# Attention with its gradient: the key-side gradient Z of two key groups in the halves of one bank, four units of a block turned on TensorE, ScalarE's order written out, new lists

## The chip, the cores and the metric

The kernel runs on one core of one Trainium2 chip. The metric is the device time of one execution in microseconds (us); three runs of the kernel before gave 2305.57, 2306.34 and 2306.37. Engines are called PE (TensorE; PEld is its weight load), ACT (ScalarE), DVE (VectorE), POOL (GpSimd) and SP (SyncE, which here mostly issues transfers).

## The reference

A block of a transformer, forward and backward, in bfloat16: sequence 2048, width 512, 32 heads of 16. The part that the change touches is attention.

```python
q, k, v = qkv[0], qkv[1], qkv[2]
scores = jnp.einsum("bhqd,bhkd->bhqk", q, k) * (Dh ** -0.5)
p = _softmax(scores, axis=-1)
o = jnp.einsum("bhqk,bhkd->bhqd", p, v)
...
_out, _vjp = jax.vjp(_f, A_x, A_wqkv, A_wo, B_w1, B_b1, B_w2, B_b2)
_grads = _vjp(grad_out)
```

Around it stand a layer norm, a gated MLP and the gradients of all weights; the kernel computes those ahead of attention and behind it.

## The kernel before

**The three parts.** A first part (up to about 157 us, and then mixed into the first block of attention) prepares operands. Attention runs to about 1949 us. A last part computes the weight gradients.

**Attention's loop.** Heads are taken in 16 pairs, and the 2048 queries in 4 groups of 512: 64 blocks. A block walks over the keys in 16 *steps* of 128 keys (`g` counts steps over all blocks, `kb = g % 16`), and both heads of the pair (`hj`) are done side by side. In one step, with the names of the lists:

- `s`: PE computes the scores, keys on partitions, two matmuls of 32 contraction rows each, in a buffer of two PSUM banks (L1058). `S`: ACT takes the exponential, which gives `et` (L1086).
- `d0`, `d1`: PE computes the output gradient times V for the first and the second head (L1080), each into a bank of its own. `m0`, `m1`: DVE multiplies each by `et`, which gives the halves of `gts` (L1097).
- `a1`, `a2`: PE accumulates in X (one bank, 128 partitions) what the queries need: from `et` with Lc and NAT (L1117, L1120; four matmuls of 32 columns each, in the four column quarters of the array), and from `gts` (L1130; two, in the upper two quarters).
- Every two steps SP issues a transfer that transposes `gts` into `gk` (L1106).

When a block's steps are done, DVE copies X to `xs`, PE transposes it (`XT`, L1142), DVE copies it out (`xt`), and `sm` (`emit_finish`) computes with small operations on DVE (rL, dl, ndr: L1163, L1166, L1168) and Pool (L1158 to L1179) the matrices W1 and W2 and the rows of the output and of dQ.

Then follows the key side, Z, for that block, while the next block's steps run. It needs the exponentials with queries on partitions, in 16 *units* (a group of 512 keys, `kc`, times a group of 128 queries, `qb`). There are two ways to get them. In 13 of the 16, PE computes the scores again, the other way round (`t`, L1070), and ACT takes the exponential (`T`, L1091). In the other three (`turned=(0, 1, 2)`: the unit `qb == 3` of the key groups 0, 1 and 2) PE transposes parts of four `et` (`E`, L1042: 8 transposes of 128x128) and DVE copies them out (`eE`, L1047), so ACT has nothing to do. `ze` and `zg` then multiply with W1 and W2 and add up in Z (L1190, L1198): two matmuls each, of 128 rows and 32 columns, in column quarters 0 and 1. Z has 64 partitions and one bank and holds 512 keys; after its four `qb`, DVE adds it to `acc` (L1213, L1215) or, in the last query group, writes the sum to `ob` (L1217), which SP stores (L1219).

**What sets the order.** PE, ACT and DVE each run a list. `PE_ORDER` and `DVE_ORDER` are written out by hand for one block; an item such as `d1:5` is the operation and its step relative to the block, and `unrolled` repeats the list with the step moved on by 16. For `t`, `T`, `ze`, `zg` and `acc` the number counts units, and units 16 to 31 belong to the block of steps 0 to 15. ACT's list is made by a loop: S, then T, of each number. The first block has its own lists (`first_block`), with the rest of the first part between its items. Each engine runs its list strictly in order, and waits for what the next item needs.

**Where items meet.** `s` and `t` share two buffers of two banks (pool `ps_st`), so the n-th of them on PE waits for ACT to finish the one two earlier. `d0` and `d1` have one buffer each, so each waits for the product of the step before. XT, E and Z all use the one bank of the tag `z` (pool `ps_z`): each *tenant* must be copied out by DVE before PE writes the next. `et` has 8 buffers, `gts` 4 (two steps each), `gk` 6 (four steps each).

Of the kernel before, what the change touches and what calls it, by code (L numbers as in the profile page):

```python
# [944 lines left out]
a2:-1 zg:-7 d1:1 t:1 ze:-6 s:2 d0:1 zg:-6 ze:-5 zg:-5 t:2 d1:2 a1:0 s:3 d0:2 XT:-1 d1:3 s:4 a1:1 a1:2 t:4 d0:3 a2:0 ze:-4  # L945
a2:1 zg:-4 a2:2 ze:-3 s:5 d1:4 zg:-3 ze:-2 t:5 d0:4 zg:-2 ze:-1 zg:-1 s:6 d1:5 a1:3 a1:4 d0:5 t:6 E:3 s:7 a1:5 d0:6 s:8
d1:6 ze:0 a2:3 zg:0 ze:1 a2:4 t:8 d1:7 zg:1 s:9 d0:7 d1:8 ze:2 a2:5 d0:8 t:9 zg:2 s:10 d1:9 ze:3 a1:6 zg:3 t:10 d0:9 a1:7
a1:8 s:11 d1:10 E:7 s:12 d0:10 a1:9 d1:11 t:12 a1:10 a2:6 ze:4 a2:7 s:13 d0:11 zg:4 d1:12 a2:8 ze:5 d0:12 t:13 zg:5 a2:9
ze:6 a2:10 d1:13 s:14 d0:13 zg:6 a1:11 d1:14 t:14 a2:11 ze:7 zg:7 s:15 d0:14 a1:12 a2:12 d1:15 t:15 E:11 s:16 d0:15 a1:13
d1:16 t:16 a1:14 a2:13 ze:8 a2:14 zg:8 s:17 d0:16 a1:15 ze:9  # L950
"""
DVE_ORDER = """
m0:-5 m1:-4 m0:-4 m1:-3 m0:-3 m1:-2 acc:-9 m0:-2 m1:-1 eE:-5 m0:-1 m1:0 m0:0 xs:-1 m1:1 m0:1 acc:-5 m1:2 m0:2 xt:-1 m1:3
m0:3 sm:-1 m1:4 m0:4 acc:-1 m1:5 m0:5 eE:3 m1:6 m0:6 m1:7 m0:7 m1:8 m0:8 m1:9 acc:3 m0:9 m1:10 eE:7 m0:10 m1:11
# [14 lines left out]
def attention_core(ctx, tc, opnds, ps_z, tail, NAT_s, NATQ_s, Oall, dQall, dKVT_out, ident_f32, ident_bf, npairs=16, nqc=4, turned=(0, 1, 2)):  # L969
# [4 lines left out]
    nc = tc.nc  # L974
# [4 lines left out]
    etp = ctx.enter_context(tc.tile_pool(name="etp", reuse_waits="tile", bufs=8))  # L979
    gtp = ctx.enter_context(tc.tile_pool(name="gtp", reuse_waits="tile", bufs=4))  # L980
    gbp = ctx.enter_context(tc.tile_pool(name="gbp", reuse_waits="tile", bufs=6))
    ep = ctx.enter_context(tc.tile_pool(name="ep", reuse_waits="tile", bufs=8))
    eep = ctx.enter_context(tc.tile_pool(name="eep", reuse_waits="tile", bufs=4))
# [38 lines left out]
    st_s = {}; st_d = {}; st_t = {}; st_et = {}; st_e = {}; st_gts = {}  # L1022
# [6 lines left out]

    def b_unit(g):  # L1030
        j = g // 16 - 1
        return (j, (g % 16) // 4, g % 4) if 0 <= j < NB else None

    def is_turned(kc, qb):
        return kc in turned and qb == 3

    def emit_E(g):

        ET = ps_z.tile([128, 2, 512], bf16, name="ET", tag="z")
        for hj in range(2):  # L1040
            for m in range(4):
                nc.tensor.transpose(ET[:, hj, m * 128:(m + 1) * 128], st_et[g - 3 + m][:, hj, 384:512], ident_bf[:])  # L1042
        cur["ET"] = ET

# [28 lines left out]
    def emit_d(g, hj):  # L1073
        j, kb = divmod(g, 16)
        p, qc = blocks[j]
        op = cur_op[p]
        d = ps_d.tile([128, 512], f32, name=f"d{hj}", tag=f"d{hj}")
        st_d[g, hj] = d
        r = slice(64 + 32 * hj, 96 + 32 * hj)
        nc.tensor.matmul(d[:], lhsT=op["KVT"][r, kb * 128:(kb + 1) * 128], rhs=op["QDT"][r, qc * 512:(qc + 1) * 512],  # L1080
                         start=True, stop=True, tile_position=(64 + 32 * hj, 0))
# [11 lines left out]
    def emit_mult(g, hj):  # L1093
        if g // 2 not in st_gts:
            st_gts[g // 2] = gtp.tile([128, 2, 2, 512], bf16, name="gts")
        gts = st_gts[g // 2]
        nc.vector.tensor_tensor(out=gts[:, g % 2, hj], in0=st_d.pop((g, hj))[:], in1=st_et[g][:, hj], op=ALU.mult)  # L1097
# [52 lines left out]
    def emit_finish(j):  # L1150
# [12 lines left out]
        nc.vector.reciprocal(out=rL[:], in_=XTv[:, :, 2:4, 17:18])  # L1163
        nc.gpsimd.tensor_tensor(out=W1[:, :, :, 0:16], in0=ndo, in1=rL[:].to_broadcast([128, 4, 2, 16]), op=ALU.mult)  # L1164
        dl = finp.tile([128, 4, 2, 1], f32, name="dl")
        nc.vector.tensor_tensor(out=dl[:], in0=XTv[:, :, 2:4, 0:1], in1=rL[:], op=ALU.mult)  # L1166
        ndr = finp.tile([128, 4, 2, 1], f32, name="ndr")
        nc.vector.scalar_tensor_tensor(out=ndr[:], in0=dl[:], scalar=-1.0, in1=rL[:], op0=ALU.mult, op1=ALU.mult)  # L1168
# [5 lines left out]
        nc.gpsimd.tensor_tensor(out=t1[:], in0=XTv[:, :, 0:2, 0:16], in1=dl[:].to_broadcast([128, 4, 2, 16]), op=ALU.mult)  # L1174
        nc.gpsimd.tensor_tensor(out=t1[:], in0=XTv[:, :, 2:4, 1:17], in1=t1[:], op=ALU.subtract)
# [6 lines left out]

    def emit_ze(g):
        j, kc, qb = b_unit(g)
        if qb == 0:
            cur["Z"] = ps_z.tile([64, 512], f32, name="Z", tag="z")
        Z = cur["Z"]
        e = st_e.pop(g)
        for hj in range(2):
            nc.tensor.matmul(Z[32 * hj:32 * hj + 32, :], lhsT=blk[j]["W1"][:, qb, hj, :], rhs=e[:, hj, :],  # L1190
                             start=(qb == 0), stop=False, tile_position=(0, 32 * hj))

    def emit_zg(g):
        j, kc, qb = b_unit(g)
        gk = blk[j]["Gk"][kc]
        for hj in range(2):
            grhs = gk[:].rearrange("q a (r h b) k -> q a r h b k", r=2, h=2)[:, :, :, hj, qb, :]
            nc.tensor.matmul(cur["Z"][32 * hj:32 * hj + 32, :], lhsT=blk[j]["W2"][:, qb, hj, :], rhs=grhs,  # L1198
                             start=False, stop=(qb == 3), tile_position=(0, 32 * hj))

    def emit_acc(g):
        j, kc, qb = b_unit(g)
        p, qc = blocks[j]
        Z = cur.pop("Z")
        if kc == 0:
            if qc == 0:
                cur["acc"] = accp.tile([64, S], f32, name="acc")
            if qc == nqc - 1:
                cur["ob"] = outp.tile([64, S], bf16, name="ob")
        ks = slice(kc * 512, (kc + 1) * 512)  # L1210
        acc = cur["acc"]
        if qc == 0:
            nc.vector.tensor_copy(out=acc[:, ks], in_=Z[:])  # L1213
        elif qc < nqc - 1:
            nc.vector.tensor_tensor(out=acc[:, ks], in0=Z[:], in1=acc[:, ks], op=ALU.add)  # L1215
        else:
            nc.vector.tensor_tensor(out=cur["ob"][:, ks], in0=Z[:], in1=acc[:, ks], op=ALU.add)  # L1217
            if kc == 3:
                nc.sync.dma_start(out=dKVT_out[p * 64:(p + 1) * 64, :], in_=cur["ob"][:])  # L1219
        if kc == 3:  # L1220
            blk[j].pop("Gk")
# [3 lines left out]
    def turned_step(g):  # L1225
        return g % 16 % 4 == 3 and g % 16 // 4 in turned

    def unrolled(order):
        items = [x.split(":") for x in order.split()]
        items = [(k, int(r)) for k, r in items]  # L1230
        late = ("t", "T", "ze", "zg", "acc")
        return [(k, 16 * b + r) for b in range(-2, NB + 3) for k, r in items
                if (16 if k in late else 0) <= 16 * b + r < (NSTEP + 16 if k in late else NSTEP)]

    def first_block():

# [36 lines left out]
    def needs(k, g):  # L1273
        if k == "V":
            return [("eE", g - 1)] if ("E", g - 1) in issued else []
# [14 lines left out]
        if k in ("E", "XT"):  # L1290
            return [("S", g) if k == "E" else ("xs", g)] + ([before[k, g]] if (k, g) in before else [])
# [4 lines left out]
        if k in ("m0", "m1"):  # L1296
            return [("S", g), ("d" + k[1], g)]
        return {"acc": [("zg", g)], "xs": [("a1", g), ("a2", g)], "xt": [("XT", g)], "sm": [("xt", g)],
                "eE": [("E", g)], "zg": [("ze", g)]}[k]

    def emit_left(g, place):
        for f, a in left[g][place]:
# [148 lines left out]
```

## Time and profile before

| | us |
|---|---|
| median of three runs | 2306.34 |
| the profiled execution | 2310.21 |
| its span, first to last instruction | 2308.3 |
| first `s` to first XT | 157.3 to 214.3 |
| first XT to last XT (64 of them) | 214.3 to 1932.3 |
| last store of `ob` issued | 1949.1 |
| mean of one `d`, product, S, T, E transpose | 0.384, 0.684, 1.043, 1.042, 0.221 |

A group of instructions in the profile has a line, an engine, an operation, the tiles out and in, their shapes, how often it occurred, the engine's busy time in it, the mean of one, and the idle time ahead of it with what ended it. Means are of single instructions; since an engine starts the next one before the last is finished, the pace at which they follow one another is shorter, and is read from the timeline (start, duration, engine, line, operation, tiles). In the table by stages, "PEclk" is the clock that TensorE was granted, as a share of its full clock, and "DMA share" the mean busy share of the transfer engines, counted by packets, so that it can exceed 1.

### The profile page before, as it was taken

The page shows a single profiled execution, that of the slowest core. Times are in us where ns is not written, and L with a number is a line of the kernel's source. Part 1 is how long each engine was busy: PE and PEld are TensorE (multiplying, and loading weights), DVE is VectorE, ACT ScalarE, POOL GpSimd, SP SyncE. Part 2 cuts the span into 40 slices and gives each one's busy share as a digit, 9 for nine tenths or more (in the row PEclk, how much of TensorE's full clock was granted, in tenths as well). Part 3 has the DMA queues.
Part 4 walks back from the last instruction along what each step waited for, and adds up shares of the span by engine and source line. Part 5 has one row for each costly group of instructions (what it writes and reads, how often), then busy time and mean ns, then how long its engine had stood idle before and what let it go on. Part 6 is the DMA issues. An engine that isn't in the chain of part 4 may idle for free.

```text
span 2308.3 us, 50925 instructions
## 1 busy us (share of the span) xinstructions
PE 2227.2 (96%) x20089; PEld 797.6 (35%) x20135; DVE 2040.3 (88%) x3612; ACT 2030.4 (88%) x2322; POOL 345.4 (15%) x808
## 2 busy tenths in 40 slices
PE   7988999999999999999999999999999998799999
PEld 3432333333333333333333333333333333344544
DVE  7767999999999999999999999999999996788355
ACT  7667999999999999999999999999999997586243
POOL 4321111111111111111111111111111112310000
PEclk9999999999999999999999999999999999899999
DMA  9888899999999999999999999999999897987872
GB/s 293 273 271 177 157 181 164 185 163 183 162 180 166 179 165 179 167 177 173 171 177 167 175 168 181 164 185 162 179 166 179 157 159 183 259 184 153 129 202 71
DMA packets 1311407, 413.46 MB, mean 179 GB/s; under 512 B 1272416, under 2 KB 1286368, under 8 KB 1310528
## 3 DMA queue, kind: packets, MB, share of 16 engines
q1 hardware_dynamic: 1302880, 391.99, 90.7%
q0 software_dynamic: 4368, 12.98, 1.7%
q10 hardware_dynamic: 3920, 5.24, 0.7%
q8 instruction: 157, 2.57, 0.5%
q14 instruction: 82, 0.67, 0.1%
HBM read 44.42 MB, written 49.03 MB: 40 GB/s over the span
## 4 chain that ended last, share of the span: by engine, by line
PE 81%; DVE 11%; ACT 3%; DMA 3%; issue 2%; SPq 0%; POOL 0%; DVEq 0%; ACTq 0%; POOLq 0%
PE d L1080 12%; PE X L1117 11%; PE s L1058 11%; PE Z L1198 9%; PE X L1130 7%; DVE gts L1097 5%; PE Z L1190 5%; PE ET L1042 5%; PE t L1070 4%; PE ps_dw L783 2%; PE ps_dy L866 2%; PE XT L1142 2%; PE X L1120 1%; PE ps_dhg L799 1%; PE ps_dwkv L899 1%
## 5 line engine op out<-in xcount | busy, mean ns | idle before, releaser
L1097 DVE TENSOR_TENSOR gts<-d,et 128x512 bf16<-128x512 f32 x2048 | 1321.8, 684 | 73.1 <-issue 22.0
L1086 ACT ACTIVATE et<-s 128x1024 bf16<-128x1024 f32 x1024 | 1042.9, 1043 | 7.6 <-PE d L1080 7.1
L1091 ACT ACTIVATE e<-t 128x1024 bf16<-128x1024 f32 x832 | 866.1, 1042 | 24.9 <-PE t L1070 6.0
L1080 PE MATMUL d<-QDT,KVT 32*128 32x512 bf16 x2048 | 757.2, 384 | 20.2 <-DVE gts L1097 15.7
L1058 PE MATMUL s<-QDT,KVT 32*128 32x512 bf16 x2048 | 398.2, 385 | 2.5 <-ACT et L1086 2.0
L1198 PE MATMUL Z<-gk,W 128*32 128x512 bf16 x2048 | 397.5, 385 | 0.0
L1117 PE MATMUL X<-et,Lc 128*32 128x512 bf16 x2048 | 370.0, 389 | 0.0
L1120 PE MATMUL X<-et,NAT 128*32 128x512 bf16 x2048 | 369.0, 388 | 0.0
L1130 PE MATMUL X<-gts,NAT 128*17 128x512 bf16 x2048 | 330.7, 381 | 0.0
L1190 PE MATMUL Z<-e,W 128*32 128x512 bf16 x1664 | 321.8, 383 | 3.9 <-DVE ob L1217 1.2
L1070 PE MATMUL t<-KVT,QDT 32*128 32x512 bf16 x1664 | 323.6, 383 | 1.0 <-ACT e L1091 1.0
L1080 PEld LDWEIGHTS <-KVT 32*128 32x128 bf16 x2048 | 172.9, 90 | 232.3 <-issue 231.9
L1164 POOL TENSOR_TENSOR W<-NATQd,rL 128x128 bf16<-128x128 bf16 x64 | 25.8, 403 | 1122.7 <-DVE rL L1163 1122.7
L1058 PEld LDWEIGHTS <-KVT 32*128 32x128 bf16 x2048 | 105.9, 91 | 250.8 <-issue 231.2
L1198 PEld LDWEIGHTS <-W 128*32 128x32 bf16 x2048 | 100.4, 95 | 173.3 <-issue 143.0
L1190 PEld LDWEIGHTS <-W 128*32 128x32 bf16 x2048 | 105.3, 94 | 107.9 <-issue 97.3
L1070 PEld LDWEIGHTS <-QDT 32*128 32x128 bf16 x1664 | 92.2, 91 | 145.7 <-issue 141.1
L1117 PEld LDWEIGHTS <-Lc 128*32 128x32 bf16 x2048 | 83.5, 93 | 162.7 <-issue 162.6
L1047 DVE COPY eE<-ET 128x1024 bf16<-128x1024 bf16 x192 | 130.2, 678 | 4.5 <-PE ET L1042 4.4
L1042 PE MATMUL ET<-ident_bf,et 128*128 128x128 bf16 x1536 | 119.4, 221 | 2.1 <-DVE e L291 2.1
L1042 PEld LDWEIGHTS <-et 128*128 128x128 bf16 x1536 | 86.8, 98 | 45.7 <-issue 45.7
L1130 PEld LDWEIGHTS <-NAT 128*17 128x17 bf16 x2048 | 79.6, 89 | 59.7 <-issue 43.3
(213 smaller groups left out, 2354.2 us busy)
## 6 DMA issues: line engine op xcount, KB each, us to landing
gk<-gts SPq DMA_TRANSPOSE x512, 4.6
H1T_s<-h1p SPq DMA_DIRECT2D x28, 256.0 KB, 4.7
h<-H1T_s SPq DMA_DIRECT2D x28, 256.0 KB, 3.6
HGT_s<-hgT SPq DMA_DIRECT2D x21, 256.0 KB, 4.3
NAT_s<-NS SPq DMA_DIRECT2D x4, 1056.0 KB, 5.3
dKVT_s<-ob SPq DMA_DIRECT2D x16, 256.0 KB, 3.5
gb<-GB_s SPq DMA_DIRECT2D x8, 512.0 KB, 5.2
Rkv<-dKVT_s SPq DMA_DIRECT2D x2, 2048.0 KB, 10.2
```

The source lines that it names most:

```text
L1042: nc.tensor.transpose(ET[:, hj, m * 128:(m + 1) * 128], st_et[g - 3 + m][:, hj, 384:512], ident_bf[:])
L1058: nc.tensor.matmul(s[:, hj, :], lhsT=op["KVT"][r, kb * 128:(kb + 1) * 128], rhs=op["QDT"][r, qc * 512:(qc + 1) * 512], start=True, stop=Tr ...
L1070: nc.tensor.matmul(t[:, hj, :], lhsT=op["QDT"][r, q0:q0 + 128], rhs=op["KVT"][r, kc * 512:(kc + 1) * 512], start=True, stop=True, tile_pos ...
L1080: nc.tensor.matmul(d[:], lhsT=op["KVT"][r, kb * 128:(kb + 1) * 128], rhs=op["QDT"][r, qc * 512:(qc + 1) * 512], start=True, stop=True, til ...
L1086: nc.scalar.activation(out=et[:], in_=st_s.pop(g)[:], func=ACT.Exp)
L1091: nc.scalar.activation(out=e[:], in_=st_t.pop(g)[:], func=ACT.Exp)
L1097: nc.vector.tensor_tensor(out=gts[:, g % 2, hj], in0=st_d.pop((g, hj))[:], in1=st_et[g][:, hj], op=ALU.mult)
L1117: nc.tensor.matmul(X[64 + 32 * hj:96 + 32 * hj, :], lhsT=Lc[:, :], rhs=et[:, hj, :], start=(kb == 0), stop=False, skip_group_check=True, t ...
L1120: nc.tensor.matmul(X[32 * hj:32 * hj + 32, :], lhsT=NATt[:, kb, hj, 1:33], rhs=et[:, hj, :], start=(kb == 0), stop=(kb == 15), tile_positi ...
L1130: nc.tensor.matmul(X[64 + 32 * hj:64 + 32 * hj + 17, :], lhsT=NATt[:, kb, hj, 0:17], rhs=gts[:, kb % 2, hj, :], start=False, stop=(kb == 1 ...
L1190: nc.tensor.matmul(Z[32 * hj:32 * hj + 32, :], lhsT=blk[j]["W1"][:, qb, hj, :], rhs=e[:, hj, :], start=(qb == 0), stop=False, tile_positio ...
L1198: nc.tensor.matmul(cur["Z"][32 * hj:32 * hj + 32, :], lhsT=blk[j]["W2"][:, qb, hj, :], rhs=grhs, start=False, stop=(qb == 3), tile_positio ...
```

## The change

- **Z.** A Z tile has 128 partitions; its lower half takes an even key group, its upper half the odd one next to it (column quarters 2 and 3). The units of two key groups alternate: unit r of a block is key group `2 * (r // 8) + r % 2`, query group `r % 8 // 2`. There are two Z tiles a block in place of four, and two `acc` in place of four, each 128 partitions wide; `ob` is stored with two transfers.
- **Turned units.** Four of 16 (`turned=(6, 7, 14, 15)`: query group 3 of every key group): 12 `t` and `T`, four `E` and `eE` a block.
- **Orders.** `PE_ORDER` and `DVE_ORDER` are new, and ACT has a list too.
- **d.** The two halves of d are one tile, still written and waited for by halves. In two of 16 steps (`m:31`, `m:32`, that is steps 15 and 0) DVE makes one product of 128x1024 of both halves.
- **Small operations.** dl and ndr move to Pool, with the sign put into dl (`nrL`, `ndl`, `ndr`); DVE keeps the reciprocal. Pool's order behind the reciprocal becomes nrL, first half of W1, ndl, W2, ndr, output rows, second half of W1, and the rest.
- **Buffers.** `et` 10, `gk` 7, `eE` 6 (before: 8, 6, 4).

```diff
 PE_ORDER = """
-a2:-1 zg:-7 d1:1 t:1 ze:-6 s:2 d0:1 zg:-6 ze:-5 zg:-5 t:2 d1:2 a1:0 s:3 d0:2 XT:-1 d1:3 s:4 a1:1 a1:2 t:4 d0:3 a2:0 ze:-4
-a2:1 zg:-4 a2:2 ze:-3 s:5 d1:4 zg:-3 ze:-2 t:5 d0:4 zg:-2 ze:-1 zg:-1 s:6 d1:5 a1:3 a1:4 d0:5 t:6 E:3 s:7 a1:5 d0:6 s:8
-d1:6 ze:0 a2:3 zg:0 ze:1 a2:4 t:8 d1:7 zg:1 s:9 d0:7 d1:8 ze:2 a2:5 d0:8 t:9 zg:2 s:10 d1:9 ze:3 a1:6 zg:3 t:10 d0:9 a1:7
-a1:8 s:11 d1:10 E:7 s:12 d0:10 a1:9 d1:11 t:12 a1:10 a2:6 ze:4 a2:7 s:13 d0:11 zg:4 d1:12 a2:8 ze:5 d0:12 t:13 zg:5 a2:9
-ze:6 a2:10 d1:13 s:14 d0:13 zg:6 a1:11 d1:14 t:14 a2:11 ze:7 zg:7 s:15 d0:14 a1:12 a2:12 d1:15 t:15 E:11 s:16 d0:15 a1:13
-d1:16 t:16 a1:14 a2:13 ze:8 a2:14 zg:8 s:17 d0:16 a1:15 ze:9
+s:-26 a2:-30 d0:-28 d1:-27 s:-25 a2:-29 ze:-32 ze:-31 zg:-32 zg:-31 d1:-26 s:-24 ze:-30 ze:-29 d0:-27 s:-23 a2:-28 zg:-30
+zg:-29 d1:-25 t:-23 d0:-26 ze:-28 ze:-27 a2:-27 zg:-28 s:-22 d1:-24 zg:-27 ze:-26 d0:-25 s:-21 zg:-26 ze:-25 zg:-25 a1:-27
+s:-20 d1:-23 d0:-24 a1:-26 a2:-26 a2:-25 a1:-25 t:-22 d1:-22 E:-25 d0:-23 t:-21 a2:-24 d1:-21 s:-19 a1:-24 a1:-23 d0:-22 t:-20
+E:-18 a1:-22 d0:-21 d1:-20 s:-18 a1:-21 a1:-20 ze:-24 ze:-23 t:-19 d0:-20 zg:-24 a2:-23 s:-17 d1:-19 zg:-23 d0:-19 t:-16
+a2:-22 ze:-22 a2:-21 ze:-21 d1:-18 t:-15 d0:-18 a2:-20 zg:-22 zg:-21 ze:-20 s:-16 zg:-20 ze:-19 zg:-19 ze:-18 d1:-17 s:-15
+d0:-17 ze:-17 zg:-18 a2:-19 t:-14 zg:-17 a1:-19 s:-14 d1:-16 d0:-16 a1:-18 a1:-17 a2:-18 a2:-17 s:-13 d1:-15 t:-13 d0:-15
+XT:-17 t:-12 d1:-14 a1:-16 a1:-15 d0:-14 s:-12 a2:-16 a2:-15 a1:-14 d1:-13 t:-11 E:-10 s:-11 d0:-13 a1:-13 a1:-12 t:-8 d1:-12
+E:-17
+"""
+ACT_ORDER = """
+T:0 T:1 S:0 S:1 T:2 S:2 S:3 T:3 T:4 S:4 T:5 S:5 T:8 S:6 S:7 S:8 S:9 T:9 S:10 S:11 S:12 T:10 T:11 S:13 T:12 S:14 T:13 S:15
 """
 DVE_ORDER = """
-m0:-5 m1:-4 m0:-4 m1:-3 m0:-3 m1:-2 acc:-9 m0:-2 m1:-1 eE:-5 m0:-1 m1:0 m0:0 xs:-1 m1:1 m0:1 acc:-5 m1:2 m0:2 xt:-1 m1:3
-m0:3 sm:-1 m1:4 m0:4 acc:-1 m1:5 m0:5 eE:3 m1:6 m0:6 m1:7 m0:7 m1:8 m0:8 m1:9 acc:3 m0:9 m1:10 eE:7 m0:10 m1:11
+m0:25 m1:27 m0:26 eE:30 m0:27 m1:28 m0:28 m1:29 m0:29 m1:30 m0:30 m:31 acc:31 m:32 xs:31 m1:33 m0:33 m1:34 xt:31 m0:34 sm:31
+m1:35 eE:38 m0:35 m1:36 eE:31 m1:37 m0:36 m1:38 m0:37 m1:39 m0:38 m1:40 m0:39 acc:39 m1:41 m0:40 m1:42 eE:39
 """
...
-def attention_core(ctx, tc, opnds, ps_z, tail, NAT_s, NATQ_s, Oall, dQall, dKVT_out, ident_f32, ident_bf, npairs=16, nqc=4, turned=(0, 1, 2)):
+def attention_core(ctx, tc, opnds, ps_z, tail, NAT_s, NATQ_s, Oall, dQall, dKVT_out, ident_f32, ident_bf, npairs=16, nqc=4, turned=(6, 7, 14, 15)):
...
+    def kc_of(r):
+        return 2 * (r // 8) + r % 2
     def b_unit(g):
-        j = g // 16 - 1
-        return (j, (g % 16) // 4, g % 4) if 0 <= j < NB else None
-    def is_turned(kc, qb):
-        return kc in turned and qb == 3
+        j, r = divmod(g - 16, 16)
+        return (j, kc_of(r), r % 8 // 2) if 0 <= j < NB else None
+    dd = ps_d.tile([128, 2, 512], f32, name="d")
     def emit_E(g):
+        b, r = divmod(g, 16)
+        qs = slice(r % 8 // 2 * 128, r % 8 // 2 * 128 + 128)
         ET = ps_z.tile([128, 2, 512], bf16, name="ET", tag="z")
         for hj in range(2):
             for m in range(4):
-                nc.tensor.transpose(ET[:, hj, m * 128:(m + 1) * 128], st_et[g - 3 + m][:, hj, 384:512], ident_bf[:])
+                nc.tensor.transpose(ET[:, hj, m * 128:(m + 1) * 128], st_et[16 * b + 4 * kc_of(r) + m][:, hj, qs], ident_bf[:])
         cur["ET"] = ET
...
-        d = ps_d.tile([128, 512], f32, name=f"d{hj}", tag=f"d{hj}")
-        st_d[g, hj] = d
+        d = dd[:, hj]
...
-        nc.vector.tensor_tensor(out=gts[:, g % 2, hj], in0=st_d.pop((g, hj))[:], in1=st_et[g][:, hj], op=ALU.mult)
+        if hj == 2:
+            nc.vector.tensor_tensor(out=gts[:, g % 2], in0=dd[:], in1=st_et[g][:], op=ALU.mult)
+        else:
+            nc.vector.tensor_tensor(out=gts[:, g % 2, hj], in0=dd[:, hj], in1=st_et[g][:, hj], op=ALU.mult)
...
         nc.vector.reciprocal(out=rL[:], in_=XTv[:, :, 2:4, 17:18])
+        nrL = finp.tile([128, 4, 2, 1], f32, name="nrL")
+        nc.gpsimd.tensor_scalar(out=nrL[:], in0=rL[:], scalar1=-1.0, scalar2=None, op0=ALU.mult)
+        ndl = finp.tile([128, 4, 2, 1], f32, name="ndl")
+        nc.gpsimd.tensor_tensor(out=ndl[:], in0=XTv[:, :, 2:4, 0:1], in1=nrL[:], op=ALU.mult)
+        ndr = finp.tile([128, 4, 2, 1], f32, name="ndr")
+        nc.gpsimd.tensor_tensor(out=ndr[:], in0=ndl[:], in1=rL[:], op=ALU.mult)
         nc.gpsimd.tensor_tensor(out=W1[:, :, :, 0:16], in0=ndo, in1=rL[:].to_broadcast([128, 4, 2, 16]), op=ALU.mult)
-        dl = finp.tile([128, 4, 2, 1], f32, name="dl")
-        nc.vector.tensor_tensor(out=dl[:], in0=XTv[:, :, 2:4, 0:1], in1=rL[:], op=ALU.mult)
-        ndr = finp.tile([128, 4, 2, 1], f32, name="ndr")
-        nc.vector.scalar_tensor_tensor(out=ndr[:], in0=dl[:], scalar=-1.0, in1=rL[:], op0=ALU.mult, op1=ALU.mult)
...
+    def z_rows(kc, hj):
+        return 64 * (kc % 2) + 32 * hj
     def emit_ze(g):
         j, kc, qb = b_unit(g)
-        if qb == 0:
-            cur["Z"] = ps_z.tile([64, 512], f32, name="Z", tag="z")
+        if g % 8 == 0:
+            cur["Z"] = ps_z.tile([128, 512], f32, name="Z", tag="z")
         Z = cur["Z"]
         e = st_e.pop(g)
         for hj in range(2):
-            nc.tensor.matmul(Z[32 * hj:32 * hj + 32, :], lhsT=blk[j]["W1"][:, qb, hj, :], rhs=e[:, hj, :],
-                             start=(qb == 0), stop=False, tile_position=(0, 32 * hj))
+            z = z_rows(kc, hj)
+            nc.tensor.matmul(Z[z:z + 32, :], lhsT=blk[j]["W1"][:, qb, hj, :], rhs=e[:, hj, :],
+                             start=(qb == 0), stop=False, tile_position=(0, z))
     def emit_zg(g):
         j, kc, qb = b_unit(g)
         gk = blk[j]["Gk"][kc]
         for hj in range(2):
+            z = z_rows(kc, hj)
             grhs = gk[:].rearrange("q a (r h b) k -> q a r h b k", r=2, h=2)[:, :, :, hj, qb, :]
-            nc.tensor.matmul(cur["Z"][32 * hj:32 * hj + 32, :], lhsT=blk[j]["W2"][:, qb, hj, :], rhs=grhs,
-                             start=False, stop=(qb == 3), tile_position=(0, 32 * hj))
+            nc.tensor.matmul(cur["Z"][z:z + 32, :], lhsT=blk[j]["W2"][:, qb, hj, :], rhs=grhs,
+                             start=False, stop=(qb == 3), tile_position=(0, z))
...
-    act = []
-    for g in range(NSTEP + 16):
-        if g < NSTEP:
-            act.append(("S", g))
-        if g >= 16 and not turned_step(g):
-            act.append(("T", g))
+    act = unrolled(ACT_ORDER)
     place = {x: i for i, x in enumerate(act)}
-    tenants = [x for x in pe if x[0] in ("XT", "E") or (x[0] == "ze" and x[1] % 4 == 0)]
-    leaves = {"XT": lambda g: ("xt", g), "E": lambda g: ("eE", g), "ze": lambda g: ("acc", g + 3)}
+    tenants = [x for x in pe if x[0] in ("XT", "E") or (x[0] == "ze" and x[1] % 8 == 0)]
+    leaves = {"XT": lambda g: ("xt", g), "E": lambda g: ("eE", g), "ze": lambda g: ("acc", g + 7)}
...
+        if k == "m":
+            return [("S", g), ("d0", g), ("d1", g)]
...
-                    issued.add((k, g))
+                    issued.update([("m0", g), ("m1", g)] if k == "m" else [(k, g)])
```

More of the change, by code (lines that the diff above doesn't have):

```diff
@@ L978, in attention_core @@
     ps_x = ctx.enter_context(tc.tile_pool(name="ps_x", reuse_waits="tile", bufs=1, space=PSUM))
-    etp = ctx.enter_context(tc.tile_pool(name="etp", reuse_waits="tile", bufs=8))
+    etp = ctx.enter_context(tc.tile_pool(name="etp", reuse_waits="tile", bufs=10))
     gtp = ctx.enter_context(tc.tile_pool(name="gtp", reuse_waits="tile", bufs=4))
-    gbp = ctx.enter_context(tc.tile_pool(name="gbp", reuse_waits="tile", bufs=6))
+    gbp = ctx.enter_context(tc.tile_pool(name="gbp", reuse_waits="tile", bufs=7))
     ep = ctx.enter_context(tc.tile_pool(name="ep", reuse_waits="tile", bufs=8))
-    eep = ctx.enter_context(tc.tile_pool(name="eep", reuse_waits="tile", bufs=4))
+    eep = ctx.enter_context(tc.tile_pool(name="eep", reuse_waits="tile", bufs=6))
     xsp = ctx.enter_context(tc.tile_pool(name="xsp", reuse_waits="tile", bufs=1))
@@ L1021, in attention_core @@
     NSTEP = NB * 16
-    st_s = {}; st_d = {}; st_t = {}; st_et = {}; st_e = {}; st_gts = {}
+    st_s = {}; st_t = {}; st_et = {}; st_e = {}; st_gts = {}
     blk = [dict() for _ in range(NB + 1)]
@@ L1076, in emit_d @@
         op = cur_op[p]
-        d = ps_d.tile([128, 512], f32, name=f"d{hj}", tag=f"d{hj}")
-        st_d[g, hj] = d
+        d = dd[:, hj]
         r = slice(64 + 32 * hj, 96 + 32 * hj)
-        nc.tensor.matmul(d[:], lhsT=op["KVT"][r, kb * 128:(kb + 1) * 128], rhs=op["QDT"][r, qc * 512:(qc + 1) * 512],
+        nc.tensor.matmul(d, lhsT=op["KVT"][r, kb * 128:(kb + 1) * 128], rhs=op["QDT"][r, qc * 512:(qc + 1) * 512],
                          start=True, stop=True, tile_position=(64 + 32 * hj, 0))
@@ L1173, in emit_finish @@
         t1 = finp.tile([128, 4, 2, 16], f32, name="t1")
-        nc.gpsimd.tensor_tensor(out=t1[:], in0=XTv[:, :, 0:2, 0:16], in1=dl[:].to_broadcast([128, 4, 2, 16]), op=ALU.mult)
-        nc.gpsimd.tensor_tensor(out=t1[:], in0=XTv[:, :, 2:4, 1:17], in1=t1[:], op=ALU.subtract)
+        nc.gpsimd.tensor_tensor(out=t1[:], in0=XTv[:, :, 0:2, 0:16], in1=ndl[:].to_broadcast([128, 4, 2, 16]), op=ALU.mult)
+        nc.gpsimd.tensor_tensor(out=t1[:], in0=XTv[:, :, 2:4, 1:17], in1=t1[:], op=ALU.add)
         rL4 = finp.tile([128, 4, 2, 1], f32, name="rL4")
@@ L1204, in emit_acc @@
         Z = cur.pop("Z")
-        if kc == 0:
+        half = g % 16 // 8
+        if half == 0:
             if qc == 0:
-                cur["acc"] = accp.tile([64, S], f32, name="acc")
+                cur["acc"] = accp.tile([128, S // 2], f32, name="acc")
             if qc == nqc - 1:
-                cur["ob"] = outp.tile([64, S], bf16, name="ob")
-        ks = slice(kc * 512, (kc + 1) * 512)
+                cur["ob"] = outp.tile([128, S // 2], bf16, name="ob")
+        ks = slice(half * 512, (half + 1) * 512)
         acc = cur["acc"]
@@ L1217, in emit_acc @@
             nc.vector.tensor_tensor(out=cur["ob"][:, ks], in0=Z[:], in1=acc[:, ks], op=ALU.add)
-            if kc == 3:
-                nc.sync.dma_start(out=dKVT_out[p * 64:(p + 1) * 64, :], in_=cur["ob"][:])
-        if kc == 3:
+            if half == 1:
+                for h in range(2):
+                    nc.sync.dma_start(out=dKVT_out[p * 64:(p + 1) * 64, :].rearrange("r (a x c) -> r a x c", a=2, x=2)[:, :, h, :],
+                                      in_=cur["ob"][64 * h:64 * h + 64].rearrange("r (a c) -> r a c", a=2))
+        if half == 1:
             blk[j].pop("Gk")
@@ L1225, in turned_step @@
     def turned_step(g):
-        return g % 16 % 4 == 3 and g % 16 // 4 in turned
+        return g % 16 in turned
     def unrolled(order):
@@ L1231, in unrolled @@
         late = ("t", "T", "ze", "zg", "acc")
+        assert len(set(items)) == len(items)
         return [(k, 16 * b + r) for b in range(-2, NB + 3) for k, r in items
@@ L1241, in first_block @@
             p.append(("s", g + 2))
-            if g % 4 == 0 and g and g // 4 - 1 in turned:
-                p.append(("E", g - 1))
+            if g in early:
+                p.append(("E", early[g]))
             p += [("d1", g + 1), ("d0", g + 1), ("a1", g), ("V", g)]
@@ L1248, in first_block @@
             v += [("m1", g), ("m0", g)]
-            if ("E", g - 1) in p:
-                v.append(("eE", g - 1))
+            if g in early:
+                v.append(("eE", early[g]))
         return p, v
+    early = {}
+    for r in turned:
+        g = 4 * kc_of(r) + 4
+        while g in early:
+            g += 1
+        if g < 14:
+            early[g] = r
     def joined(first, rest):
-        done = set(first)
+        done = set(first) | {("m", g) for k, g in first if k == "m0"}
         return first + [x for x in rest if x not in done]
@@ L1274, in needs @@
         if k == "V":
-            return [("eE", g - 1)] if ("E", g - 1) in issued else []
+            return [("eE", early[g])] if g in early else []
         if k == "W":
@@ L1290, in needs @@
         if k in ("E", "XT"):
-            return [("S", g) if k == "E" else ("xs", g)] + ([before[k, g]] if (k, g) in before else [])
+            return [("S", g - g % 16 + 4 * kc_of(g % 16) + 3) if k == "E" else ("xs", g)] + ([before[k, g]] if (k, g) in before else [])
         if k == "S":
@@ L1306, in attention_core @@
               "ze": emit_ze, "zg": emit_zg, "XT": lambda g: emit_XT(g // 16), "E": emit_E, "S": emit_exp_a, "T": emit_exp_b,
-              "m0": lambda g: emit_mult(g, 0), "m1": lambda g: emit_mult(g, 1), "acc": emit_acc, "xs": lambda g: emit_xs(g // 16),
+              "m0": lambda g: emit_mult(g, 0), "m1": lambda g: emit_mult(g, 1), "m": lambda g: emit_mult(g, 2), "acc": emit_acc, "xs": lambda g: emit_xs(g // 16),
               "V": lambda g: emit_left(g, 0), "W": lambda g: emit_left(g, 1), "xt": lambda g: emit_xt(g // 16), "sm": lambda g: emit_finish(g // 16), "eE": emit_eE}
@@ L1318, in attention_core @@
                     act_of[k](g)
-                    issued.add((k, g))
+                    issued.update([("m0", g), ("m1", g)] if k == "m" else [(k, g)])
                     at[n] += 1
                     moved = True
-                    if k in ("m0", "m1") and g % 2 == 1 and ("m0", g) in issued and ("m1", g) in issued:
+                    if k in ("m", "m0", "m1") and g % 2 == 1 and ("m0", g) in issued and ("m1", g) in issued:
                         emit_dmat(g)
```

## The prediction

> **What bounds the kernel now.** I read the page's first two parts, then the table by stages, then the groups by shape, then the timelines of TensorE (PE), ScalarE (ACT) and VectorE (DVE) in the middle of the attention stage. The page's head, and two stretches of the stage:
>
> ```profile
> span 2308.3 us, 50925 instructions
> PE 2227.2 (96%) x20089; PEld 797.6 (35%) x20135; DVE 2040.3 (88%) x3612; ACT 2030.4 (88%) x2322; POOL 345.4 (15%) x808
> ```
> ```profile
> core 0: us, PE busy (x) PEld busy (x) DVE busy (x) ACT busy (x) POOL busy (x), PEclk, DMA share, GB/s
> 600.00:900.00 300.00, 297.17 (x3069) 98.04 (x3066) 287.93 (x486) 296.61 (x321) 40.50 (x111) 1.00 1.02 175
> ```
> In the stage PE, ACT and DVE are busy 99, 99 and 96%: no engine alone can be sped up with profit. The stage is a loop: XT (L1142) starts at 599.24 and, seven blocks later, at 789.56, so a block takes **27.19 us**. There are 64 blocks; from the first XT (214.3) to the last (1932.3) are 63 periods. What each engine needs for a block is read from the pace of its instructions, since the busy time covers overlaps. ACT's timeline:
>
> ```profile
> 639.76 1.96 ACT L1086 ACTIVATE et<-s 128x1024 bf16<-128x1024 f32 x2
> 641.57 1.07 ACT L1091 ACTIVATE e<-t 128x1024 bf16<-128x1024 f32 x1
> 642.48 1.08 ACT L1086 ACTIVATE et<-s 128x1024 bf16<-128x1024 f32 x1
> 643.69 1.02 ACT L1091 ACTIVATE e<-t 128x1024 bf16<-128x1024 f32 x1
> ```
> Two exponentials from 639.76 to 641.57 are 0.905 us each; the step from 642.48 to 643.69 is 1.21, so 0.3 us were lost there. 29 a block (16 S, 13 T) need 29 x 0.905 = **26.25**; 0.94 us are lost. DVE's timeline:
>
> ```profile
> 627.91 1.29 DVE L1097 TENSOR_TENSOR gts<-d,et 128x512 bf16<-128x512 f32 x2
> 629.12 0.19 DVE L1163 RECIPROCAL rL<-xt 128x8 f32<-128x8 f32 x1
> 629.34 0.37 DVE L1166 TENSOR_TENSOR dl<-xt,rL 128x8 f32<-128x8 f32 x1
> 629.75 0.52 DVE L1168 SCALAR_TENSOR_TENSOR ndr<-dl,rL 128x8 f32<-128x8 f32 x1
> ```
> Two products take 1.21, so 0.605 each, and the copies keep the same pace. A block has 32 products, 3 eE, 4 acc, xs and xt: 41 x 0.605 = 24.8, with the three small ones (0.62 us at 1010.70, 1.07 us here) **25.4 to 25.9**. PE's timeline:
>
> ```profile
> 627.01 0.39 PE L1058 MATMUL s<-QDT,KVT 32*128 32x512 bf16 x2
> 627.33 0.39 PE L1117 MATMUL X<-et,Lc 128*32 128x512 bf16 x2
> 627.34 0.39 PE L1120 MATMUL X<-et,NAT 128*32 128x512 bf16 x2
> 627.56 0.38 PE L1117 MATMUL X<-et,Lc 128*32 128x512 bf16 x2
> ...
> 628.48 0.38 PE L1130 MATMUL X<-gts,NAT 128*17 128x512 bf16 x2
> 628.49 0.38 PE L1198 MATMUL Z<-gk,W 128*32 128x512 bf16 x2
> 628.69 0.38 PE L1130 MATMUL X<-gts,NAT 128*17 128x512 bf16 x2
> 628.70 0.39 PE L1190 MATMUL Z<-e,W 128*32 128x512 bf16 x2
> 629.02 0.39 PE L1058 MATMUL s<-QDT,KVT 32*128 32x512 bf16 x2
> ```
> Neighbours in different column quarters (Lc with NAT, a2 with a Z pair) start together: one group. A group after a group of the same shape follows by 0.22; a change between s/t/d (32 rows) and X/Z (128 rows) takes 0.32 either way. E takes 0.555, XT 0.585.
>
> **PE, by counting.** I grouped both lists so (neighbours in free quarters join). Before: 52 changes x 0.32, 24 x 0.22, and 3 E and 1 XT with 0.32 ahead of each: 16.6 + 5.3 + 2.6 + 0.9 = **25.5**. After: 45 x 0.32, 26 x 0.22, 4 E, 1 XT: 14.4 + 5.7 + 3.5 + 0.9 = **24.5**. Of 18 Z pairs that stood alone, 6 are left; ten groups now hold two Z pairs (ze with ze, zg with ze), while a2 with Z falls from 14 to 6. One t pair goes and 8 transposes come.
>
> **ACT.** One T a block goes: 28 x 0.905 = **25.34**, a fall of 0.905. Nothing else of ACT's work moves; its order only names which of S and T comes first.
>
> **DVE.** 28 single products, 4 eE, 2 acc (128 partitions wide at the same 512 columns; the 64-wide ones cost 680 ns, as the 128-wide xs does), xs and xt: 36 x 0.605 = 21.8. The two joined products (128x1024 from PSUM) have no row; the nearest are the eE copy of 128x1024 at 0.678 and two single ones at 2 x 0.684 = 1.37. I take two paces, 1.21 each, since the float input is the same. With the reciprocal 0.2: **24.4**. The Trainium skill (Perfetto Trace Analysis, Optimizing Scalar/DVE Operations) puts some 125 ns of fixed cost on each DVE instruction on PSUM; by that a joined one would be an estimated 1.09 and the sum 24.2. DVE would still not be the bound.
>
> **The small operations.** dl and ndr leave DVE: 0.34 us at their shortest (167 ns each), 0.85 at 629.34, where Pool was copying KPad; I count 0.4. Their three successors on Pool lie between the 128x8 row there (237 ns) and the 128x128 rows (403 ns): 0.7 to 1.2 us on an engine that is 13% busy. They lie ahead of W1: rL to W1 becomes some 2.2 us (seven steps of 0.24 to 0.40). In the new list the XT of the same block stands about 6 us of PE work ahead of the first ze; XT, xt, a product and rL take 2.3 of it, so 1.5 us cover the chain. The Trainium skill (SBUF — State Buffer, Who interferes with whom) says that a DVE operation with two SBUF inputs and a Pool operation that reads SBUF shut each other out. It agrees with dl at 0.37 beside the KPad copy against 0.17 without it; by it the operations moved to Pool cannot hold up DVE's products, and the gain would be the longer figure.
>
> **What the sums leave out.** Before lost 0.94 beyond ACT's need; I look for it in the list. *First,* s and t share two buffers, so PE must hand over one per 0.905; a lag up to about 0.4 is hidden (0.905 less 0.39 for the pair and 0.1 for two hand-overs). Nine gaps of either list exceed 0.905, up to 1.27 and 1.29. Adding them up along the list, with the lag never under zero, loses 0.13 a block before and 0.24 after. *Second,* a half of d is free again only after its product: 0.385 + 0.07 (d at 641.94, product at 642.40) + 0.684 + 0.04 = 1.18. Where the list sets two d of one half closer, PE waits. These shortfalls add up to 0.87 (d0) and 0.98 (d1) before, mostly at gaps of 0.63 and 0.85; after, to 0.66 and 0.50. So the list explains 1.0 to 1.1 of the 0.94 before, and 0.74 to 0.90 after. Period after: 25.34 + 0.74 to 0.90, I take **26.2**.
>
> **At nothing.** More buffers (et 10, gk 7, eE 6) cost only space; gk's lifetime in the list (up to 27 steps) fits 28. The 512 transposes on SP stay; a 1-us table shows DMA shares of 0.2 between them, so eight fit in 26.2 us. The second store of ob adds 0.5 us of SP (its row 547 ns) and counts only for the last pair. First block, and all outside attention, as before. The end is between 6 us shorter (the last Z starts four steps sooner) and 3 longer; I take 0.
>
> **The sum.** 63 x (27.19 - 26.2) = 62.4 us less. The profiled execution took 2310.2 (span 2308.3), 3.9 over the median 2306.3; it would become 2247.8, and the median **2244**.
>
> **Rivals.**
> (1) *Nothing waits for d:* only 0.24 is lost, period 25.6, 2206; at ACT's bare need 25.34, 2190. For it: every engine has over 0.8 us to spare against ACT. Against: the close d of the list.
> (2) *The joined products hold d:* each keeps both halves for 0.385 + 0.07 + 1.21 + 0.04 = 1.7, but the list has d1 again after 1.29 and d0 after 1.50, with an acc between the two: up to 0.5 a block, period 26.7, 2275. Against: only 2 of 16 steps.
> (3) *The one bank z becomes the bound, slower:* seven tenants pass through it (XT, 4 E, 2 Z), and PE stops until DVE has copied one out. From E to the next ze stand 1.6 us of PE work, against 0.62 + 0.07 + 0.68 = 1.37 if DVE is free at once. One product in the way at two of the four E costs 1.21: 27.41, 2320. It decides from 0.99 a block, 0.25 per E. Against: idle before eE and before ze is now 4.5 and 3.9 us in all.
> (4) *The Z pairs don't run side by side:* ten groups split, PE needs 24.5 + 2.2 = 26.7 and with the 1.7 that it now has above its sum 28.4: 2384. Against: Lc and NAT, four quarters of one bank, start together.
>
> **How the numbers follow.** Forecast (26.0 to 26.5, 2225 to 2262): 0.50. (1) 0.20, (2) 0.15, (3) 0.08, (4) 0.04, all eaten by waits 0.03. A measurement tells 0.2%, 4.6 us, from no change. Faster 0.84 (forecast, (1), nearly all of (2)), same 0.04, slower 0.12. The range from 2198 (most of (1)) to 2300 (the long end of (2), joined products at 1.37) leaves out 0.04 below and 0.15 above.
>
> **What would show it.** XT to XT of 26.2; S and T at 0.905 with under 1 us lost a block; ze pairs of two partition halves starting together and 0.22 apart; joined products near 1.2; no idle DVE at rL. Wrong, if PE's waits stand ahead of ze or E (case 3), if d after a joined product shows the gap (2), or if Z pairs follow one another (4).

## The result and the profile after

The changed kernel takes **3423.8 us** (median of four runs, 3395.43 to 3447.8) against 2305.95 before: ratio 1.481, interval 1.469 to 1.493. The forecast was 2244. One of the four runs was set aside as disturbed; the ratio is of the others. The profiled execution took 3395.43. Its head and a stretch of the attention stage:

```profile
span 3393.6 us, 51691 instructions
PE 2848.0 (84%) x20473; PEld 877.8 (26%) x20519; DVE 2065.8 (61%) x3293; ACT 2110.6 (62%) x2258; POOL 383.2 (11%) x1000
```
```profile
core 0: us, PE busy (x) PEld busy (x) DVE busy (x) ACT busy (x) POOL busy (x), PEclk, DMA share, GB/s
800.00:1100.00 300.00, 249.31 (x1942) 69.89 (x1940) 181.71 (x269) 192.30 (x192) 30.01 (x92) 0.76 0.56 104
```
DVE and ACT are busy 61 and 64% of the stretch (before: 96 and 99%), and TensorE's granted clock is 0.76 (before 1.00). No engine is the bound; all wait. From XT at 1025.01 to XT at 1291.25 are six blocks of **44.4 us** on average (they alternate between 43.2 and 45.6), where 27.19 were needed before: 63 x 17.2 is 1084 us, nearly all of the difference. Whom they wait for, in the table of waits (engine, line, releaser: us in total, times, longest); before:

```profile
PE d L1080 <- DVE gts L1097: 15.7, 68, 0.8
DVE gts L1097 <- PE d L1080: 20.9, 70, 2.2
```
and after, where d has line 1089 and its single product 1109:
```profile
PE d L1089 <- DVE gts L1109: 469.1, 802, 1.9
DVE gts L1109 <- PE d L1089: 476.7, 681, 2.8
```
PE waits for products and products wait for PE. The timelines of a few us, DVE's and then PE's, show how:

```profile
1202.61 0.69 DVE L1109 TENSOR_TENSOR gts<-d,et 128x512 bf16<-128x512 f32 x1 [0.46 <-PE d L1089]
1203.82 0.69 DVE L1109 TENSOR_TENSOR gts<-d,et 128x512 bf16<-128x512 f32 x1 [0.52 <-PE d L1089]
...
1205.03 0.68 DVE L1109 TENSOR_TENSOR gts<-d,et 128x512 bf16<-128x512 f32 x1
...
1206.24 0.69 DVE L1109 TENSOR_TENSOR gts<-d,et 128x512 bf16<-128x512 f32 x1 [0.42 <-PE t L1080]
```
```profile
1203.36 0.37 PE L1089 MATMUL d<-QDT,KVT 32*128 32x512 bf16 x1
...
1204.57 0.37 PE L1089 MATMUL d<-QDT,KVT 32*128 32x512 bf16 x1 [0.29 <-DVE gts L1109]
...
1205.76 0.37 PE L1089 MATMUL d<-QDT,KVT 32*128 32x512 bf16 x1
```
The d at 1203.36 begins 0.06 us behind the end of the product of 1202.61; the product of 1203.82 begins 0.46 us behind that d; the next d 0.06 behind that product. These d are of the two halves in turn. A half should be free while the other is being multiplied; here it is not, and d and product form one chain with a link of 1.21 us: 28 single links and two joined ones for 16 steps.

The built program says why. Of 1600 matmuls into d in the middle of the stage, 1550 of the kernel before wait for exactly the product that read their own half one step earlier, and 50 for none. After, 150 do that, 150 carry no wait, and **1300 wait for a later product, one or two further on in DVE's list**, which read the other half. Products still wait for their own half's matmul alone. So in this program the framework (the language's layer that places the waits) orders a write behind all the reads of the tile so far, not of the part that is written; with one tile for both halves, that includes the other half's product. The section on the change says of the tile that it is "waited for by halves"; that holds for the products, and for the writes it is wrong.

### The profile page after: what moved, and what is told of

It is laid out like the page before. It is cut to its first block, busy times and chain, and to the rows that moved or that the text cites. A ratio compares the mean times of both kernels' runs of the same rounds, so it can differ in the third digit from the quotient of the medians.

```text
span 3393.6 us, 51691 instructions
## 1 busy us (share of the span) xinstructions
PE 2848.0 (84%) x20473; PEld 877.8 (26%) x20519; DVE 2065.8 (61%) x3293; ACT 2110.6 (62%) x2258; POOL 383.2 (11%) x1000
## 5 line engine op out<-in xcount | busy, mean ns | idle before, releaser
L1109 DVE TENSOR_TENSOR gts<-d,et 128x512 bf16<-128x512 f32 x1794 | 1233.0, 690 | 902.0 <-PE d L1089 476.7
L1089 PE MATMUL d<-QDT,KVT 32*128 32x512 bf16 x2048 | 861.4, 465 | 486.5 <-DVE gts L1109 469.1
L1100 ACT ACTIVATE e<-t 128x1024 bf16<-128x1024 f32 x768 | 785.4, 1024 | 430.7 <-PE t L1080 210.6
L1068 PE MATMUL s<-QDT,KVT 32*128 32x512 bf16 x2048 | 485.6, 471 | 2.1 <-ACT e L1100 1.4
L1217 PE MATMUL Z<-gk,W 128*32 128x512 bf16 x2048 | 472.9, 522 | 0.0
L1142 PE MATMUL X<-gts,NAT 128*17 128x512 bf16 x2048 | 446.8, 478 | 0.0
L1129 PE MATMUL X<-et,Lc 128*32 128x512 bf16 x2048 | 434.0, 475 | 0.0
L1107 DVE TENSOR_TENSOR gts<-d,et 128x1024 bf16<-128x1024 f32 x127 | 155.5, 1225 | 165.9 <-PE d L1089 121.1
L1052 PE MATMUL ET<-ident_bf,et 128*128 128x128 bf16 x2048 | 197.9, 254 | 0.9 <-DVE e L291 0.9
L1208 PE MATMUL Z<-eE,W 128*32 128x512 bf16 x512 | 153.0, 596 | 0.0
```

The source lines that it names most:

```text
L1068: nc.tensor.matmul(s[:, hj, :], lhsT=op["KVT"][r, kb * 128:(kb + 1) * 128], rhs=op["QDT"][r, qc * 512:(qc + 1) * 512], start=True, stop=Tr ...
L1089: nc.tensor.matmul(d, lhsT=op["KVT"][r, kb * 128:(kb + 1) * 128], rhs=op["QDT"][r, qc * 512:(qc + 1) * 512], start=True, stop=True, tile_p ...
L1100: nc.scalar.activation(out=e[:], in_=st_t.pop(g)[:], func=ACT.Exp)
L1109: nc.vector.tensor_tensor(out=gts[:, g % 2, hj], in0=dd[:, hj], in1=st_et[g][:, hj], op=ALU.mult)
L1129: nc.tensor.matmul(X[64 + 32 * hj:96 + 32 * hj, :], lhsT=Lc[:, :], rhs=et[:, hj, :], start=(kb == 0), stop=False, skip_group_check=True, t ...
L1142: nc.tensor.matmul(X[64 + 32 * hj:64 + 32 * hj + 17, :], lhsT=NATt[:, kb, hj, 0:17], rhs=gts[:, kb % 2, hj, :], start=False, stop=(kb == 1 ...
```

## The experiments

**1. Two tiles again.** In the changed kernel:

```diff
-... m:31 acc:31 m:32 ...
+... m1:31 m0:31 acc:31 m1:32 m0:32 ...
...
-    dd = ps_d.tile([128, 2, 512], f32, name="d")
+    st_d = {}
...
-        d = dd[:, hj]
+        st_d[g, hj] = ps_d.tile([128, 512], f32, name=f"d{hj}", tag=f"d{hj}")
+        d = st_d[g, hj][:]
...
```


> The changed kernel with the two halves of d as two tiles again, a new one each step as before, and each of the two joined products split into two single ones; all else as changed. Theory A (one tile: a matmul into one half of d waits for the newest product of either half, so d and product alternate along one chain; in the trace 0.46 us from d to product and 0.06 from product's end to the next d, 1.2 us a link): the chain is gone, a block takes 26.0 to 26.5 us as first forecast (DVE's need grows by 0.0 to 0.2), the whole 2225 to 2265 us, the granted clock is 1.00 again in the stage. Rival B (the one bank z with its tenants, or the new lists themselves, or ACT's order stall PE): hardly any fall, still above 3000 us and PE's waits move to ze and E. Rival C (the granted clock of 0.75 is the cause and comes from the Z groups of four column quarters): clock stays near 0.75, above 2800 us.

Measured: **2288.31 us**, ratio to before 0.992 (0.990 to 0.993), clock 0.986. The chain is gone, B and C with it, and in the built program 1550 of 1600 matmuls into d again wait for their own half's product and 50 for none. A's time was 23 us too low: only 18 us of the forecast 62 are left; see below. The edit changes two things, the tile and the joined products; experiments 2 and 3 change one each.

**2. The kernel before, with one tile.**

```diff
+    dd = ps_d.tile([128, 2, 512], f32, name="d")
...
-        d = ps_d.tile([128, 512], f32, name=f"d{hj}", tag=f"d{hj}")
-        st_d[g, hj] = d
+        d = dd[:, hj]
...
```


> The kernel before with only the two halves of d put into one tile that is allocated once; lists, Z, turned units and small operations as before. Theory A: the chain appears here too; 32 links of about 1.2 us and the copies that fall between them, 38 to 46 us a block, 3000 to 3450 us, with the clock falling below 0.9 because PE waits. Rivals B and C: nothing of theirs is in this kernel, so 2300 to 2320 us at a clock of 0.99.

Measured: **3193.58 us** (1.384, 1.381 to 1.388), 41.1 us a block, clock 0.872. Theory A: putting the halves into one tile costs 887 us by itself.

**3. One tile, joined products split.** (`m:31` and `m:32` as in 1, d as changed.)

> The changed kernel with only the two joined products split into single ones; d stays one tile. Theory A: the chain of 32 links stays, 3250 to 3450 us. Rival D (the joined products alone, which hold both halves, cause the alternation): near 2250 us.

Measured: 3663.47 us (1.588). D falls, and A's number was too low: split, the products make a block longer. In the profiled executions it takes 48.5 in place of 44.3 us on average. The two links that are saved when the products are joined are worth only 4 x 1.21 - 2 x 1.75 = 1.3 us of these 4.2 (a joined link is 0.46 + 1.225 + 0.06); the stage's granted clock is also lower, 0.68 in place of 0.76, and the rest was not parted.

**4. Two tiles, allocated once.**

```diff
-    dd = ps_d.tile([128, 2, 512], f32, name="d")
+    dh = [ps_d.tile([128, 512], f32, name=f"d{h}", tag=f"d{h}") for h in range(2)]
...
-        d = dd[:, hj]
+        d = dh[hj][:]
...
```
The joined products are split as in 1.


> As the first of these, but the two tiles of d are allocated once and not each step. Theory A (what counts is that the halves share a tile): as the first, 2225 to 2265 us. Rival E (what counts is that the tile is allocated once, so that no new buffer's release names the right product): as the changed kernel, above 3000 us.

Measured: 2289.54 us, as the first. What counts is that the halves share a tile, not when it is allocated. (A was 25 us too low here, much as in 1.)

**Where the rest of the gain went.** The first experiment's blocks, XT copy to XT copy, in the middle of the stage: 26.29, 26.61, 27.27, 31.58, 26.29, 26.28, 29.43, 27.51, 26.28, 26.29, 26.33, 27.58 us. The undisturbed period is **26.28**, against the 26.2 forecast; two of every four blocks, at the change of the pair of heads, are longer. In the longest, DVE's first wait by size, then SP's queue ahead of it:

```profile
DVE gts L1107 <- DMA gk<-gts: 2.4, 1, 2.4
```
```profile
750.38 2.10 SPq L1018 DMA_TRANSPOSE KVT<-KPad  x1
752.91 3.55 SPq L1021 DMA_TRANSPOSE QDT<-QPad  x1
756.57 4.73 SPq L1116 DMA_TRANSPOSE gk<-gts  x2
...
761.40 1.34 SPq L1239 DMA_DIRECT2D dKVT_s<-ob  x2
```
Two operand transposes and two stores stand among gts's own transposes, 7 us of the queue. A gts buffer comes free only when its transpose has read it; the product waits, and PE with it. PE's timeline and the table by stages, just behind:

```profile
769.95 0.37 PE L1090 MATMUL d<-QDT,KVT 32*128 32x512 bf16 x1 [1.61 <-DVE gts L1107]
...
774.54 0.60 PE L1090 MATMUL d<-QDT,KVT 32*128 32x512 bf16 x1
775.08 0.61 PE L1127 MATMUL X<-et,Lc 128*32 128x512 bf16 x2
```
```profile
740.00:766.00 26.00, 25.66 (x284) 8.79 (x281) 24.46 (x41) 25.82 (x29) 3.59 (x12) 1.00 1.16 196
770.00:779.00 9.00, 8.77 (x68) 3.00 (x71) 6.66 (x11) 4.29 (x5) 0.00 (x0) 0.62 0.93 182
```
After the wait d lasts 0.60 in place of 0.37 and the mean granted clock is 0.62 for 9 us; in a table by single us it is 0.50 from 772 to 778. PE waited 1.8 us in all in this block, and the block is 5.3 us longer than an undisturbed one; the clock missing from 771 to 779 adds up to 3.4 us, which is about the rest. The Trainium skill (TensorE: Matmul & The Clock Gate, What's actually happening) describes a clock that is halved after an idle window of some 3.4 us; the trace agrees with the halving (0.50), though PE's longest single wait here was 1.6 us.

**5. Five buffers of gts** in place of four, on top of 1 (`bufs=4` to `bufs=5` of the pool `gtp`).

> The changed kernel with two tiles for d and split products (as the first experiment, 2288 us), and with 5 buffers of gts in place of 4. Seen in that run: undisturbed blocks take 26.28 us, but two of every four, at the change of the pair of heads, take 27 to 31; there SP's queue holds the transposes of KPad and QPad and the stores of ob among gts's own transposes, a product then waits up to 2.4 us for a gts buffer, PE idles and its clock halves for about 8 us. Theory F (the release of gts by the delayed transposes): 10 steps of cover in place of 8, 3.3 us more, so most of the 43 us lost comes back: 2246 to 2262 us, and no product waits for a transfer. Rival G (the delay reaches PE through gk, which Z reads, or through the loads of the pair's operands): 2283 to 2292 us.

Measured: **2260.07 us** (0.980, 0.979 to 0.981), 28 us below the first, within F's range. No product waits for a transfer in the 900 us looked at. The transfers are as dense as before (DMA share 1.03 from 600 to 1500 us, 1.01 in experiment 1); a fifth buffer is enough to hide them from the products.

Some 13 us of blocks above 26.28 are left, and another wait makes most of them. Pool's rows and then PE's in the longest block (29.18 us):

```profile
829.36 0.67 POOL L1010 COPY KPad<-NAT 128x544 bf16<-128x544 bf16 x1 [7.42 <-DMA NAT<-NAT_s]
...
830.54 0.24 POOL L1175 TENSOR_SCALAR nrL<-rL 128x8 f32<-128x8 f32 x1
...
832.14 0.40 POOL L1181 TENSOR_TENSOR W<-NATQq,ndr 128x128 bf16<-128x128 bf16 x1
```
```profile
832.59 0.40 PE L1206 MATMUL Z<-e,W 128*32 128x512 bf16 x4 [1.65 <-POOL W L1181]
```
DVE has rL ready at 827.4, but on Pool the copy of KPad stands first and waits for the load of NAT, so nrL starts 3.2 us late, and `ze` waits for W1. Nine blocks at changes of the pair have such a wait, 0.45 to 1.65 us, and these nine hold 10 of the 13 us. So rival G's second way, through the loads of the pair's operands, is real too, though its price was not. A Pool list with the small operations ahead of the copy was not tried.

**6. Loads further apart** (`if g % 3 == 0 and load_q` to `g % 8`).

> As the first experiment (2288 us), but the five steps of loading the next pair are issued eight steps apart in place of three, so the two large transposes stand in the queue some 13 us apart. Theory F: each large transpose alone still delays gts by some 2.5 us, and the block has 8 transposes of 3.3 us of transfer pace already, so about half of the 43 us comes back: 2255 to 2275 us. Rival G: 2283 to 2292 us.

Measured: 2288.48 us. A miss that tells nothing of F: SP's order came out the same as in 1, with the two transposes 2.5 us apart (745.65 and 748.14), because the framework, not this line, places them: SP's instructions stand in the same order in both built programs. The run repeats the first.

**7. Both 5 and 6.**

> Both: 5 buffers of gts and loads eight steps apart. Theory F: the least of the four, 2240 to 2255 us, nearly all blocks at 26.3 us. Rival G: 2280 to 2292 us.

Measured: 2259.35 us (0.980): as 5, for the reason given at 6, and 4 us above F's range.

**8. Small operations back on DVE**, on top of 1 (`emit_finish` as in the kernel before).

> As the first experiment (2288 us), but the small operations as before: dl and ndr on DVE, their sign and Pool's order too. By the prediction they are not on the path (DVE had 1.8 us a block to spare): 2284 to 2300 us, undisturbed blocks 26.2 to 26.5. Rival (DVE's pace is what leaves 0.94 us a block above ACT's need): 0.6 us a block more, 26.9, 2320 us or above.

Measured: 2289.75 us, undisturbed blocks 26.45. They cost 0.17 us a block, not 0.6, and nothing that the whole time shows: the blocks that are longer than the plain ones lose some 37 us here and some 44 in 1.

**9. More work for PE in the chain.**

```diff
-        for hj in range(2):
+        for hj in (0, 1, 0, 1):
```
in `emit_s` and `emit_t` of the changed kernel.

> The changed kernel (d one tile, joined products) in which PE computes every s and every t pair twice into the same buffer: 28 groups of 0.22 us more PE work a block, 6.2 us at the full clock, the results the same. Theory H (part of the 44.4 us of a block is the clock: 81 of 189 single d in a 300-us stretch last 0.6 us in place of 0.37, since PE waits so much that it is granted half its clock): with more to do the granted clock rises above 0.85, and the time falls or stays, 3150 to 3400 us, although there is more work. Rival I (the chain of d and products alone sets the time, at any clock): the work either fits into PE's idle time, 3390 to 3450 us, or adds up to 6.2 us a block, up to 3800 us.

Measured: 3552.64 us; clock 0.819 in place of 0.788. The clock rose less than H wanted and the time grew; in the profiled executions a block takes 46.9 in place of 44.3 us. It fits I, but does not part the two, as the extra work lengthened the chain too. What the trace gives for d alone: its mean is 465 ns in place of 384, and 32 of them would be 2.6 us a block. That is no bound, since PE's other work between the links slows down with it.

**10. Control: the kernel before with five gts.**

> The kernel before with 5 buffers of gts in place of 4 and nothing else, as a control of the second finding. Theory F: its blocks of 27.18 us leave SP's transposes enough time, only some 0.3 us is lost in every fourth block, so at most 5 us come back: 2300 to 2307 us. Rival J (a fifth buffer helps any of these kernels by as much): 2278 us.

Measured: 2306.43 us, ratio 1.0002 (0.9992 to 1.0012). At 27.18 us a block the four buffers are enough, and J falls; in the first experiment, with a period of 26.28, the fifth is worth 28 us.

## Why the prediction was wrong, point by point

- **The step that failed** is the second item of "What the sums leave out": "a half of d is free again only after its product". It was carried over to the changed kernel with a new list of gaps, as if the two kernels had the same rule. With one tile a half is free only behind the newest product of either half. By the link of 1.21, 28 x 1.21 and two joined ones of 0.46 + 1.225 + 0.06 are 37.4 us; measured were 44.4. In the six blocks the single links whose d lasted 0.37 took 1.18 on average, and those whose d lasted about 0.60 (10.5 a block) took 1.66: some 4 of the remaining 7 us lie among the single links, in stretches of halved clock, and some 3 at the joined products. Whether the clock is the cause there, or the PE work that stands between product and d, was not parted. No rival held it: (2) came nearest, but priced only the joined products, which in truth shorten the block (experiment 3). Nothing forecast a time near 3400; the slower cases ended at 2384.
- **The grouping in the PE sum held.** Z groups of four quarters run side by side: in experiment 1 two `ze` pairs, four matmuls of 0.39, take 0.40 us together at 931.08. Of the first two lines each spans two groups: single matmuls start at 929.98 (`ze` with a2), 930.20 (`ze` with `zg`) and 930.41 (`zg`), 0.22 apart. Rival (4) falls. Whether PE needs 24.5 us a block no run shows. The lines:

```profile
929.98 0.59 PE L1206 MATMUL Z<-e,W 128*32 128x512 bf16 x4
930.21 0.59 PE L1215 MATMUL Z<-gk,W 128*32 128x512 bf16 x4
...
931.08 0.40 PE L1206 MATMUL Z<-e,W 128*32 128x512 bf16 x4
```
- **The period without the chain held in size:** 26.28 against 26.2 in the undisturbed blocks of experiments 1 and 5. What is lost beyond ACT's 25.34 is 0.94 there, the same as before; that the new list loses less, 0.74 to 0.90, is not borne out, and its working from gaps was not tested by itself. The joined product lasted 1.225; the next copy starts 1.14 behind it at the shortest (1110.95 and 1112.09 in the changed kernel), and that is the pace to set against the 1.21 taken and the estimated 1.09. The undisturbed blocks are of kernels with split products, so the joined ones without the chain were not tried.
- **Rival (3)**, the bank z, did not appear: in 900 us of experiment 5 PE's largest wait by group is 7.8 us, XT for xs.
- **The small operations** are nearly off the path in plain blocks (0.17 us a block, experiment 8); the three on Pool took 0.20 to 0.24. But the 1.5 us of cover was not always there: at a change of pair Pool waits for NAT and copies KPad first, and `ze` waited up to 1.65 us for W1 (experiment 5, at 832.59).
- **"At nothing" was mis-sized.** "Eight fit in 26.2 us" held for plain blocks and not where two more transposes and two stores join them. Price: 28 us (experiment 5 against 1). Of what puts 2260 above 2244, some 5 us are of the period (63 x 0.08) and some 13 of blocks that still take 26.4 to 29.2, most of them at changes of pair; the end behind the last XT, taken at no change, was some 5 us shorter (371 in place of 376).

## What to carry to other kernels

Before merging two buffers into one tile, ask what the framework releases: a part, or the whole. Here two tiles that alternate between two engines became one chain when they were one tile; the lists and the sums showed nothing of it, while the program's waits do. A shorter period is a new load for every queue beside it: count its buffers again for the worst block, not for the plain one, and look at what stands first in an engine's list there. In experiment 1 the price of a stall on TensorE was more than its length (5.3 us for 1.8), with a granted clock of 0.50 behind it.

## What the runs showed of the hardware

- A wait of 1.6 us on TensorE was followed by 9 us at a mean granted clock of 0.62, six of them at 0.50 (experiment 1). With waits spread over the whole stage, PE 83% busy, the mean was 0.76 (changed kernel), with a d of 0.60 in place of 0.37 us in the slow stretches; without the chain it was 0.99 (experiment 1).
- A VectorE product of 128x1024 from two banks took 1225 ns on average, and one of 128x512 690, in the changed kernel: 155 ns less than two.
- The best version, experiment 5 (the change with two tiles for d, split products and five gts buffers), beats both kernels: 2260.07 us, 0.980 of before (0.979 to 0.981).
